# A fused attention and channel-mix kernel: batch 4's denominators by turns on VectorE too, gate-mix products and late memory keys and values on ScalarE, and a new order of steps

## The chip, the core and the metric

The kernel runs on one core of a Trainium2 chip. A core has a matrix engine (TensorE; the profile shows its products as PE and its weight loads as PEld), a vector engine (VectorE, DVE), a scalar engine (ScalarE, ACT), GpSimd (POOL), which here issues the input loads, and SyncE (SP), which issues most stores. Each engine works through its own queue in order; semaphores tie the queues together. The metric is device time in microseconds, the median of repeated executions.

## What is computed

Eight batches of eight heads, 576 positions of 64 dimensions, and 32 memory slots per head:

```python
a = exp(phi - max(phi)); a = a / (sum(a, over positions) + 1e-9)    # 8 x 8 x 576 x 32
k_m = einsum('bhsm,bhsd->bhmd', a, k);  v_m = einsum('bhsm,bhsd->bhmd', a, v)
scores = q @ k_m.T / 8
attn = exp(scores - max) / (sum(exp, over memory slots) + 1e-9)
x = (attn @ v_m), heads side by side                                # 8 x 576 x 512
x_prev = x shifted by one position, zero first
xk = mu_k * x + (1 - mu_k) * x_prev;  xr = mu_r * x + (1 - mu_r) * x_prev
kk = relu(xk @ w_k) ** 2                                            # d_ff = 1024
out = sigmoid(xr @ w_r) * (kk @ w_v)                                # float32
```

The large products are `xk @ w_k`, `kk @ w_v` and `xr @ w_r`. The kernel computes in bf16 with float32 sums, and leaves out the maxima.

## The kernel before

The order of the whole kernel is written out by hand in `PLAN` (line 19), a list of words. Each word is one step, and the steps issue their instructions in this order; an engine's queue is what the words put on it, one after the other. A word is `who:what`. `p:` is a load of weights or of the first two batches, `c0:` to `c8:` key tiles, `g:` gates, `sg:` pairs of gates, `o:` outputs, and a bare number is a step of that batch's attention. The batches run in the order 0, 1, 2, 3, 4, 5, 7, 6 up to the scores, and every step of a later batch is woven into the channel mix of earlier ones.

Attention of batch b: `exp` (line 227, ScalarE) makes exp(phi) from the loaded float32. `z` (line 249) sums it over positions by nine small products, and VectorE takes the reciprocal `rz` (line 252). `kv` (line 239) is 72 small products that give both memory keys and values in PSUM; for batches 0 and 1 keys and values are summed apart (`k`, `v`), for batch 0 also by halves of the rows (`k0c`, `k1c`, `v0c`, `v1c`). `nk` and `nv` (lines 271 and 280) multiply keys and values by `rz` on VectorE: the division of memory keys and values. `tk` turns the keys on TensorE (line 300) and copies them back (line 305). `q0`, `q1` turn the queries on VectorE (line 318). `s` makes the scores (line 333) and their exponentials (line 338, ScalarE).

The denominators are made in one of two ways. In the first, `l0` to `l3` sum the exponentials with a block of ones on TensorE (line 348) and take the logarithm on ScalarE (line 353), and `r0z`, `r1z` (or `h0z` to `h3z`) take exp(-log) (line 358). In the second, "by turns", VectorE turns the exponentials in 32 by 32 blocks (`fe`, line 363), sums and inverts them (`fs`, lines 369 and 370) and turns the result back while spreading it (`fo`, line 375). Before the change batches 0 to 4 go the first way, and 5, 6, 7 the second. `w0`, `w1` weigh the exponentials (line 382).

For batches 2 to 7, `x0` and `x1` multiply with the memory values into four PSUM tiles each, which ScalarE copies to `x` (line 394). `dd` takes the differences to the position before (line 406). The mixes `k0d`, `k2d` (for keys) and `r0d`, `r2d` (for gates) multiply two 128-row blocks of the difference by mu minus one (line 416) and add `x` (line 417), all on VectorE. Batches 0 and 1 fold mu into the memory values (`nk0` to `nr1`, line 425) and make both mixes directly by products (`mk`, `mr`, lines 287 and 442). `mub` spreads mu over the partitions (line 202), and `mu` turns it (line 210).

Channel mix: a key tile (line 514) is four products of up to 512 tokens, a Relu on ScalarE (line 518) and a square on VectorE (line 522). A gate (line 537) is four products and an Exp (line 542); `sg` ends two gates with Ln and Exp (lines 548, 549). An output is eight products (line 563), one multiply on VectorE (line 565) and its store. `busy4` issues four products of zeros (line 197), which nobody reads.

All PSUM tiles come from one ring of eight, in the order of the steps: a step that takes a tile waits until the reader of the tile eight before has finished. Inputs of batch b+2 are asked for by `b:load`, in the order phi, k, v, q, on GpSimd's queue.

Of the kernel before, what the change touches and what calls it, by code (L numbers as in the profile page):

```python
# [11 lines left out]
BF16 = mybir.dt.bfloat16  # L12
# [7 lines left out]
    "p:q:0a 0:exp1 0:exp0 0:z 0:k0c 0:mub 0:qh0 p:k:0b 0:k1c p:q:0b 0:hn1 0:hn0 p:v:0b 0:ht1 0:ht0 0:s0 0:qh1 0:s1",  # L20
    "p:v:0a 0:l0 0:l1 0:l2 0:v1c 0:h1z p:wk:0-4 0:h2z 0:nr1 0:l3 0:v0c 0:y2 0:h0z 0:nk0 0:y0 0:h3z 0:y1 0:nk1",
    "p:wr:0-4 p:wk:4-8 0:busy4 0:y3 0:nr0 0:mk1 0:mk0 p:phi:1 0:mr0 c0:1b c0:2b c0:0a c0:4a 0:mr1 p:k:1 p:q:1 c0:1a",
    "1:exp c0:7b g:2 g:3 c0:4b p:v:1 p:wv:0-2 1:z 1:k sg:1 1:nk 1:q0 g:0 c0:7a c0:3a c0:6a c0:0b g:1 1:tk 1:q1 c0:2a",
    "c0:5b c0:5a 1:s 1:v 1:nr1 1:nr0 c0:3b p:wv:2-4 1:nk0 1:l1 1:nk1 0:mu c0:6b 1:l2 1:h1z 1:l0 1:h2z 1:y1 1:y2 1:l3",
    "1:h0z o:3a o:2a 1:y0 1:h3z o:2b 1:y3 sg:0 o:3b 1:mr0 1:mk0 g:5 0:load 1:mk1 g:4 2:exp c1:1 c1:6 c1:0 2:z 1:mr1",
    "o:1b 2:kv 2:nk o:0b 2:tk 2:nv 2:q0 1:load sg:2 2:q1 c1:7 c1:2 c1:4 2:s c1:3 c1:5 3:exp 2:l2 2:l0 2:l3 o:5 2:l1",
    "2:r0z 2:r1z 2:w0 3:z 2:w1 o:1a o:4 3:kv 3:nk 3:nv 2:x0 o:0a g:8 3:tk 3:q0 2:x1 3:q1 2:dd 2:k0d g:7 g:6 3:s",
    "2:load 2:k2d sg:3 o:6 2:r0d 3:l1 o:7 3:l3 3:load 2:r2d 4:exp c2:4 3:l2 c2:6 3:l0 3:r0z c2:2 3:r1z 3:w1 4:z 3:w0",
    "c2:7 c2:0 c2:3 g:9 4:kv 3:x1 4:nv 4:nk c2:1 c2:5 3:x0 5:exp 4:tk 4:q1 4:q0 g:10 3:dd sg:4 3:k0d g:11 o:9 4:s o:8",
    "3:k2d 3:r0d sg:5 o:11 5:z 5:kv 4:l3 c3:2 4:l1 5:q1 g:12 5:nk 3:r2d 4:l2 c3:5 5:q0 4:l0 4:r1z c3:3 c3:0 5:load",  # L30
    "4:r0z 4:w1 4:w0 g:13 c3:6 5:nv sg:6 5:tk 4:load c3:7 c3:4 c3:1 4:x1 o:10 7:q1 7:q0 4:x0 o:13 4:dd 7:exp o:12",
    "4:k2d g:17 g:15 7:z 4:k0d 5:s 7:kv 5:fe 7:nk 6:exp g:14 g:16 5:fs c4:0 c4:5 4:r2d 7:nv 6:z 7:tk 5:fo sg:7 o:15",
    "5:w1 sg:8 o:14 7:s 5:w0 c4:1 c4:6 c4:4 6:kv 4:r0d 5:x0 6:nk c4:2 c4:3 7:fe c4:7 6:q0 5:x1 g:19 5:dd 6:q1 o:16",
    "o:17 g:21 6:tk 6:nv 5:k2d 5:k0d 7:fs g:18 sg:9 g:20 6:s o:18 6:fe c5:0 6:fs c5:2 c5:5 c5:3 6:fo c5:6 6:w0 6:w1",
    "c5:1 c5:4 c5:7 5:r0d 5:r2d sg:10 o:19 6:x1 o:20 7:fo o:21 7:w0 g:23 6:x0 7:w1 6:load g:22 sg:11 6:dd o:22 g:24",
    "g:25 6:k0d 7:x0 6:k2d o:23 7:x1 7:dd 6:r0d g:26 7:k0d c6:2 7:k2d 7:load c6:3 6:r2d c6:1 sg:12 c6:5 c6:7 7:r2d",
    "c6:0 c6:6 c6:4 c7:1 c7:2 c7:7 c7:4 g:27 sg:13 c7:6 o:26 c7:5 7:r0d c7:0 o:25 o:24 g:29 c7:3 o:27 c8:5 c8:1 g:31",
    "c8:0 g:30 c8:2 sg:15 g:28 sg:14 c8:7 c8:6 o:31 o:30 c8:4 g:32 g:33 o:28 c8:3 o:29 sg:16 g:35 g:34 sg:17 o:33",
    "o:32 o:34 o:35",
# [11 lines left out]
def kernel(  # L51
# [13 lines left out]
    nc = tc.nc  # L65
# [147 lines left out]
    def attention(b):  # L213
# [51 lines left out]
        def norm_k(cs=(0, 1)):  # L265

            def go():
                if "kbd" not in st:
                    st["kbd"] = work.tile([128, 2, 2, 2, PB], BF16, name="kbd", tag="kbd", bufs=3)
                for c in cs:  # L270
                    nc.vector.tensor_scalar_mul(
                        st["kbd"][:, :, c],
                        st["k"][c].rearrange("m (d h) -> m h d", h=2).unsqueeze(2).to_broadcast([128, 2, 2, PB]),
                        st["rz"][:, c:c + 1])
            return go
# [344 lines left out]
```

## Time and profile before

| | |
|---|---|
| median of 3 runs | 205.29 us (205.17 to 206.56) |
| the profiled execution | 205.91 us |
| its span, first to last instruction | 204.1 us |
| TensorE busy | 187.7 us (92%) |
| VectorE busy | 147.5 us (72%), 372 instructions |
| ScalarE busy | 148.5 us (73%), 292 instructions |
| GpSimd busy | 29.4 us (14%) |
| mean granted TensorE clock | 0.997 |
| loads and stores | 31.29 MB, 153 GB/s over the span |

Busy time is the union of an engine's instructions. A product's end is modelled, so TensorE's busy time covers the flow of products through the array. In the 40 slices, a digit is the busy share of a slice in tenths. In rows of instructions in order of time, the first number is the start in us, the second the length of the stretch; a bracket tells how long the engine had been idle and what released it. In rows of groups, after the bar stand busy us, mean ns of one, and the idle time ahead with what ended it.

### The profile page before, as it was taken

To read this page: it belongs to the slowest core of one execution; us is meant where nothing else is said; L and a number is where in the kernel's file an instruction comes from. 1 tells how busy PE (TensorE), PEld (TensorE's weight loads), DVE (VectorE), ACT (ScalarE), POOL (GpSimd) and SP (SyncE) were. 2 spreads that over 40 slices of the span, in tenths; PEclk is the share of its full clock that TensorE was granted. 3 is DMA by queue.
4 is the path that set the end of the run, shared out by engine and by line. 5 is a ranking of instruction groups with operands and counts; after the bars stand their busy time and mean duration, and the time that the engine had idled before them with its cause. 6 is when DMAs were issued, how large, how long until landed. Compare 5 with 4: busy or idle time off the path is not lost.

```text
span 204.1 us, 5371 instructions
## 1 busy us (share of the span) xinstructions
PE 187.7 (92%) x2152; PEld 98.4 (48%) x2173; DVE 147.5 (72%) x372; ACT 148.5 (73%) x292; POOL 29.4 (14%) x45
## 2 busy tenths in 40 slices
PE   0469999999999999999979999999999999999992
PEld 0225666846464454454446564444434444444451
DVE  1266747848578997997499999999999948404332
ACT  2226898998869989989839982966788493696640
POOL 7652422204123010027000000000000000000000
PEclk9999999999999999999999999999999999999998
DMA  6999999999999999789999130320532002602545
GB/s 161 179 206 207 266 207 201 265 224 283 223 264 251 243 291 211 208 135 222 265 232 230 22 91 14 92 53 3 136 71 51 0 5 51 154 0 52 119 100 143
DMA packets 24537, 31.29 MB, mean 153 GB/s; under 512 B 1968, under 2 KB 19648, under 8 KB 24512
## 3 DMA queue, kind: packets, MB, share of 16 engines
q0 software_dynamic: 17392, 20.91, 54.7%
q1 hardware_dynamic: 6352, 9.19, 17.9%
q10 hardware_dynamic: 768, 0.85, 1.3%
q8 instruction: 17, 0.28, 0.6%
q14 instruction: 8, 0.07, 0.1%
HBM read 38.28 MB, written 9.44 MB: 234 GB/s over the span
## 4 chain that ended last, share of the span: by engine, by line
PE 72%; DVE 14%; DMA 7%; ACT 3%; issue 2%; DVEq 0%; POOLq 0%
PE pk L514 24%; PE pv L563 24%; PE pr L537 13%; DMA q<-in_q_dram 4%; PE kvps L239 3%; DMA kv<-in_k_dram 3%; DVE qT L318 2%; DVE sq L522 2%; PE scps L333 2%; PE mxps L287 2%; DVE se L369 1%; PE nops L287 1%; DVE mu_d L416 1%; PE zps L348 1%; DVE o L565 1%
## 5 line engine op out<-in xcount | busy, mean ns | idle before, releaser
L514 PE MATMUL pk<-xkT,wk 128*128 128x512 bf16 (+4 forms) x346 | 67.7, 341 | 0.3
L563 PE MATMUL pv<-wv,sq 128*128 128x512 bf16 (+1 forms) x320 | 66.1, 353 | 0.4
L518 ACT ACTIVATE rl<-pk 128x512 bf16<-128x512 f32 (+3 forms) x80 | 42.4, 556 | 13.1 <-PE pk L514 7.9
L522 DVE TENSOR_TENSOR sq<-rl 128x512 bf16<-128x512 bf16 (+5 forms) x104 | 31.4, 336 | 24.3 <-ACT rl L518 23.4
L514 PEld LDWEIGHTS <-wk 128*128 128x128 bf16 x352 | 33.2, 98 | 28.4 <-issue 0.9
L563 PEld LDWEIGHTS <-sq 128*128 128x128 bf16 x328 | 31.1, 98 | 29.4 <-issue 0.9
L537 PE MATMUL pr<-wr,xrT 128*128 128x512 bf16 x137 | 34.8, 380 | 0.6 <-ACT xrT L442 0.2
L542 ACT ACTIVATE sg<-pr 128x512 f32<-128x512 f32 x36 | 21.3, 603 | 17.0 <-DVE o L565 10.0
L565 DVE TENSOR_TENSOR o<-sg,pv 128x512 f32<-128x512 f32 (+1 forms) x41 | 24.6, 614 | 10.1 <-PE pv L563 9.7
L537 PEld LDWEIGHTS <-xrT 128*128 128x128 bf16 x144 | 13.3, 98 | 14.9 <-ACT xrT L442 0.6
L549 ACT ACTIVATE sg<-sg 128x1024 f32<-128x1024 f32 x18 | 19.0, 1057 | 0.6
L548 ACT ACTIVATE sg<-sg 128x1024 f32<-128x1024 f32 x18 | 19.1, 1061 | 0.2
L394 ACT CAST x<-nops 128x320 bf16<-128x320 f32 (+1 forms) x48 | 15.6, 419 | 3.0 <-PE nops L287 3.0
L338 ACT ACTIVATE e<-scps 128x288 bf16<-128x288 f32 x32 | 10.6, 417 | 7.9 <-PE scps L333 7.9
L416 DVE TENSOR_SCALAR mu_d<-diff,mu 128x576 bf16<-128x576 bf16 x48 | 15.4, 364 | 0.1
L318 DVE STREAM_TRANSPOSE qT<-q 128x576 uint32<-128x576 uint32 (+1 forms) x16 | 13.1, 837 | 2.8 <-DMA q<-in_q_dram 2.8
L382 DVE TENSOR_TENSOR atn<-e,lz 128x576 bf16<-128x576 bf16 (+2 forms) x20 | 12.3, 631 | 1.6 <-ACT lz L358 1.6
L239 PE MATMUL kvps<-kv,em 64*32 64x128 bf16 (+1 forms) x720 | 9.0, 219 | 2.7 <-DMA kv<-in_k_dram 1.8
L227 ACT ACTIVATE em<-ph 128x1152 bf16<-128x1152 f32 (+1 forms) x9 | 9.5, 1065 | 2.5 <-DMA ph<-in_phi_dram 2.5
L239 PEld LDWEIGHTS <-em 64*32 64x32 bf16 x720 | 7.6, 96 | 6.2 <-issue 6.2
L417 DVE TENSOR_TENSOR xkT<-x,mu_d 128x1152 bf16<-128x1152 bf16 x12 | 9.1, 759 | 0.4
L417 DVE TENSOR_TENSOR xrT<-x,mu_d 128x1152 bf16<-128x1152 bf16 x12 | 9.1, 759 | 0.4
(62 smaller groups left out, 136.8 us busy)
## 6 DMA issues: line engine op xcount, KB each, us to landing
out_dram<-o SPq DMA_DIRECT2D x61, 128.0 KB, 2.4
ph<-in_phi_dram POOLq DMA_DIRECT2D x7, 576.0 KB, 17.2
kv<-in_k_dram POOLq DMA_DIRECT2D x7, 576.0 KB, 18.2
q<-in_q_dram POOLq DMA_DIRECT2D x7, 576.0 KB, 20.3
kv<-in_v_dram POOLq DMA_DIRECT2D x7, 576.0 KB, 20.5
out_dram<-o SPq DMA_DIRECT2D x18, 64.0 KB, 5.7
wk<-in_moe_w_k_dram POOLq DMA_DIRECT2D x2, 512.0 KB, 13.1
wv<-in_moe_w_v_dram POOLq DMA_DIRECT2D x2, 512.0 KB, 20.6
```

The lines of the kernel that those rows point to most:

```text
L239: nc.tensor.matmul(kvps[c][g * M:(g + 1) * M], lhsT=em[ROWS[c], j, g, :], rhs=kv5[ROWS[c], parts, g, j, :], start=j == 0, stop=j == NJ - 1 ...
L416: nc.vector.tensor_scalar_mul(t[:, i], st["d"][:, pr + i, :], mu1[:, o:o + 1])
L417: nc.vector.tensor_add(dst, st["x"][:, pr:pr + n], t)
L514: nc.tensor.matmul(pk[:, p0 - lo:p1 - lo], lhsT=wk_sb[:, di, fi * 128:(fi + 1) * 128], rhs=xk_T[:, di, p0 % RING:p0 % RING + p1 - p0], sta ...
L518: nc.scalar.activation(rl, pk, AF.Relu)
L522: nc.vector.tensor_mul(sq[:, fi, p:p + p1 - p0], rl[:, p0 - lo:p1 - lo], rl[:, p0 - lo:p1 - lo])
L537: nc.tensor.matmul(pr, lhsT=xr_T[:, di, c0:c0 + 128], rhs=wr_sb[:, di, :], start=(di == 0), stop=(di == ND - 1))
L542: nc.scalar.activation(sg[:, t % 2], pr, AF.Exp, scale=-1.0)
L548: nc.scalar.activation(gated[p], gated[p], AF.Ln, bias=1.0)
L549: nc.scalar.activation(gated[p], gated[p], AF.Exp, scale=-1.0)
L563: nc.tensor.matmul(pv[:, cols], lhsT=sq[:, fi, p:p + 128], rhs=wv_sb[:, fi, cols], start=(fi == 0), stop=(fi == NF - 1))
L565: nc.vector.tensor_mul(o[:, cols], gated[t // 2][:, t % 2, cols], pv[:, cols])
```

## The change

Three parts, and a new plan around them.

1. Batch 4 has `fe`, `fs`, `fo` in place of `l0` to `l3`, `r0z`, `r1z`: its denominators are made by turns on VectorE.
2. The gate mixes of batches 4 to 7 are `r0e`, `r2e` in place of `r0d`, `r2d`: the products with mu run on ScalarE (a Copy with a scale per partition), and the add stays on VectorE.
3. Memory keys and values of batches 4 to 7 are divided by `ak`, `av` in place of `nk`, `nv`: on ScalarE as well.

The plan orders nearly all steps anew. At the start, the second half of batch 0's keys is loaded ahead of its queries; weights `wk:4-8` come ahead of `wk:0-4`, and phi of batch 1 ahead of `wr`; `mub` and `mu` are issued ahead of batch 0's sums; the head's steps `l`, `h..z`, `s0`, `s1` are woven differently; and `busy9` stands in place of `busy4`. In the middle, `7:kv` is issued ahead of `5:s`, and `7:q0`, `7:q1` behind both values steps of batch 4. Words `6:load` and `7:load` ask for nothing, since there is no batch 8 or 9. In the plan's part of the diff below, lines of "..." stand for plan lines left out.

```diff
@@ PLAN @@
-    "p:q:0a 0:exp1 0:exp0 0:z 0:k0c 0:mub 0:qh0 p:k:0b 0:k1c p:q:0b 0:hn1 0:hn0 p:v:0b 0:ht1 0:ht0 0:s0 0:qh1 0:s1",
-    "p:v:0a 0:l0 0:l1 0:l2 0:v1c 0:h1z p:wk:0-4 0:h2z 0:nr1 0:l3 0:v0c 0:y2 0:h0z 0:nk0 0:y0 0:h3z 0:y1 0:nk1",
-    "p:wr:0-4 p:wk:4-8 0:busy4 0:y3 0:nr0 0:mk1 0:mk0 p:phi:1 0:mr0 c0:1b c0:2b c0:0a c0:4a 0:mr1 p:k:1 p:q:1 c0:1a",
-    "1:exp c0:7b g:2 g:3 c0:4b p:v:1 p:wv:0-2 1:z 1:k sg:1 1:nk 1:q0 g:0 c0:7a c0:3a c0:6a c0:0b g:1 1:tk 1:q1 c0:2a",
...
-    "3:k2d 3:r0d sg:5 o:11 5:z 5:kv 4:l3 c3:2 4:l1 5:q1 g:12 5:nk 3:r2d 4:l2 c3:5 5:q0 4:l0 4:r1z c3:3 c3:0 5:load",
-    "4:r0z 4:w1 4:w0 g:13 c3:6 5:nv sg:6 5:tk 4:load c3:7 c3:4 c3:1 4:x1 o:10 7:q1 7:q0 4:x0 o:13 4:dd 7:exp o:12",
-    "4:k2d g:17 g:15 7:z 4:k0d 5:s 7:kv 5:fe 7:nk 6:exp g:14 g:16 5:fs c4:0 c4:5 4:r2d 7:nv 6:z 7:tk 5:fo sg:7 o:15",
-    "5:w1 sg:8 o:14 7:s 5:w0 c4:1 c4:6 c4:4 6:kv 4:r0d 5:x0 6:nk c4:2 c4:3 7:fe c4:7 6:q0 5:x1 g:19 5:dd 6:q1 o:16",
...
-    "c8:0 g:30 c8:2 sg:15 g:28 sg:14 c8:7 c8:6 o:31 o:30 c8:4 g:32 g:33 o:28 c8:3 o:29 sg:16 g:35 g:34 sg:17 o:33",
-    "o:32 o:34 o:35",
+    "p:k:0b 0:exp0 0:exp1 0:mub 0:mu 0:z 0:k1c 0:k0c 0:hn0 0:hn1 p:q:0a 0:qh0 0:ht0 p:q:0b p:v:0b 0:qh1 0:ht1 p:v:0a",
+    "0:s0 0:l0 0:h0z 0:s1 0:l1 0:v0c 0:y0 0:v1c 0:nr0 0:nk1 0:h1z 0:l2 0:l3 0:nr1 p:wk:4-8 0:h3z 0:y1 0:h2z 0:y3 0:y2",
+    "0:busy9 0:nk0 p:wk:0-4 0:mk1 p:phi:1 0:mk0 c0:3b p:wr:0-4 0:mr0 1:exp 0:mr1 c0:3a c0:6b c0:1b c0:4a g:3 c0:2a",
+    "c0:5b p:k:1 g:1 g:2 1:k 1:z 1:nk p:q:1 1:q0 sg:1 1:q1 c0:7b c0:6a p:v:1 c0:7a 1:tk g:0 c0:0a c0:0b c0:5a 1:s",
...
+    "3:x1 2:r2d 4:q1 4:kv 4:ak c2:4 c2:7 3:x0 4:q0 3:load g:9 sg:4 5:exp 3:dd 4:tk 4:av 3:k2d o:8 o:9 3:k0d g:12 g:10",
+    "5:z 3:r2d 3:r0d 5:q0 4:s 5:kv 5:ak 4:fe 5:av 5:q1 g:11 c3:3 c3:0 sg:5 4:fs 5:load 7:exp c3:7 4:fo c3:6 4:w0",
+    "4:load c3:4 g:13 4:w1 o:10 c3:2 sg:6 c3:5 7:z c3:1 o:11 4:x0 g:14 7:kv 4:x1 7:ak 7:q0 7:q1 g:15 5:tk 4:dd o:12",
+    "4:k2d sg:7 5:s 4:k0d 6:exp o:13 g:16 5:fe 5:fs g:17 5:fo c4:1 7:tk sg:8 o:15 7:av c4:6 c4:5 5:w0 c4:0 c4:3 5:w1",
+    "6:z 6:q0 4:r2e 7:s c4:4 7:fe 6:load c4:2 c4:7 o:14 4:r0e 5:x0 o:17 6:kv 6:ak 7:fs 5:x1 5:dd 6:q1 g:18 g:19 sg:9",
+    "o:16 5:k0d 6:av g:21 g:20 6:tk 5:k2d 5:r2e o:19 6:s o:18 6:fe 5:r0e 6:fs c5:4 6:fo c5:2 c5:1 sg:10 g:23 6:w1",
...
+    "o:24 c7:7 o:25 g:29 7:r2e sg:13 c7:5 7:r0e o:26 c8:4 c8:3 c7:4 c8:5 c8:6 c7:3 g:28 c7:2 o:27 c8:1 sg:14 g:30",
+    "g:31 sg:15 o:31 c8:0 o:30 g:32 g:33 o:28 sg:16 c8:2 o:29 c8:7 o:33 g:35 g:34 sg:17 o:32 o:34 o:35",
@@ -262,23 +261,31 @@
                     nc.vector.tensor_sub(left, left, terms[:, i])
             st["es"] = [terms[:, i] for i in range(3)]
 
-        def norm_k(cs=(0, 1)):
+        def norm_k(cs=(0, 1), by_act=False):
 
             def go():
                 if "kbd" not in st:
                     st["kbd"] = work.tile([128, 2, 2, 2, PB], BF16, name="kbd", tag="kbd", bufs=3)
                 for c in cs:
-                    nc.vector.tensor_scalar_mul(
-                        st["kbd"][:, :, c],
-                        st["k"][c].rearrange("m (d h) -> m h d", h=2).unsqueeze(2).to_broadcast([128, 2, 2, PB]),
-                        st["rz"][:, c:c + 1])
-            return go
-
-        def norm_v():
-            vb = work.tile([128, 2, D], BF16, name="vb", tag="vb", bufs=3)
-            for c in range(2):
-                nc.vector.tensor_scalar_mul(vb[:, c], st["v"][c], st["rz"][:, c:c + 1])
-            st["vb"] = vb
+                    out, kc = st["kbd"][:, :, c], st["k"][c].rearrange("m (d h) -> m h d", h=2)
+                    kc = kc.unsqueeze(2).to_broadcast([128, 2, 2, PB])
+                    if by_act:
+                        nc.scalar.activation(out, kc, AF.Copy, scale=st["rz"][:, c:c + 1])
+                    else:
+                        nc.vector.tensor_scalar_mul(out, kc, st["rz"][:, c:c + 1])
+            return go
+
+        def norm_v(by_act=False):
+
+            def go():
+                vb = work.tile([128, 2, D], BF16, name="vb", tag="vb", bufs=3)
+                for c in range(2):
+                    if by_act:
+                        nc.scalar.activation(vb[:, c], st["v"][c], AF.Copy, scale=st["rz"][:, c:c + 1])
+                    else:
+                        nc.vector.tensor_scalar_mul(vb[:, c], st["v"][c], st["rz"][:, c:c + 1])
+                st["vb"] = vb
+            return go
 
         def head_tiles(pss, src, lo, hi, cols=slice(0, None), **flags):
             for c in range(2):
@@ -407,13 +414,16 @@
                 nc.vector.tensor_copy(d[:, :, 0:1], x[:, :, 0:1])
             return go
 
-        def mix(which, pr, n=1):
+        def mix(which, pr, n=1, by_act=False):
             def go():
                 dst = (xk_T, xr_T)[which][:, pr:pr + n, x0:x0 + S]
                 t = work.tile([128, 2, S], BF16, name="mu_d", tag="mu_d")[:, :n]
                 for i in range(n):
                     o = which * ND + pr + i
-                    nc.vector.tensor_scalar_mul(t[:, i], st["d"][:, pr + i, :], mu1[:, o:o + 1])
+                    if by_act:
+                        nc.scalar.activation(t[:, i], st["d"][:, pr + i, :], AF.Copy, scale=mu1[:, o:o + 1])
+                    else:
+                        nc.vector.tensor_scalar_mul(t[:, i], st["d"][:, pr + i, :], mu1[:, o:o + 1])
                 nc.vector.tensor_add(dst, st["x"][:, pr:pr + n], t)
             return go
 
@@ -444,7 +454,7 @@
 
         two = [(0, 0), (0, 1), (1, 0), (1, 1)]
         steps = {"exp": exp_phi, "kv": ekv(slice(0, 2)), "k": ekv(slice(0, 1)), "v": ekv(slice(1, 2)),
-                 "z": esum, "nk": norm_k(), "nv": norm_v, "tk": tr_k(), "s": scores((0, 1)), "load": reload, "mu": load_mu, "mub": load_mu_b,
+                 "z": esum, "nk": norm_k(), "nv": norm_v(), "ak": norm_k(by_act=True), "av": norm_v(True), "tk": tr_k(), "s": scores((0, 1)), "load": reload, "mu": load_mu, "mub": load_mu_b,
                  "zr": sum_rows}
         steps.update(fe=fold_e, fs=fold_sum, fo=fold_out)
         for i in range(2):
@@ -473,6 +483,7 @@
             steps[f"d{2 * i}d"] = diff(2 * i, 2)
             for w in range(2):
                 steps[f"{'kr'[w]}{2 * i}d"] = mix(w, 2 * i, 2)
+                steps[f"{'kr'[w]}{2 * i}e"] = mix(w, 2 * i, 2, by_act=True)
         steps["dd"] = diff(0, 4)
         for hf in range(2):
             steps[f"x{hf}"] = values(hf)
```

## The prediction

> **What bounds the kernel now.** I read the page first, for the engine that sets the end; then the work by stages, for where that engine is not fed; then what was waited for in the two weak places; and last the groups by shape, for prices. From the page, busy time and its 40 slices:
>
> ```profile
> PE 187.7 (92%) x2152; PEld 98.4 (48%) x2173; DVE 147.5 (72%) x372; ACT 148.5 (73%) x292; POOL 29.4 (14%) x45
> ...
> PE   0469999999999999999979999999999999999992
> ...
> DVE  1266747848578997997499999999999948404332
> ACT  2226898998869989989839982966788493696640
> ```
>
> TensorE is busy 187.7 of 204.1 us; its zeros and low digits stand only at the two ends, with a 9 nearly throughout the rest. VectorE and ScalarE have 9s in other places, so each has stages of its own in which it is full. The work by stages (columns: stretch, length, then busy us and count for PE, weight loads, DVE, ACT, POOL):
>
> ```profile
> 0.00:20.00 20.00, 9.95 (x228) 5.20 (x236) 8.36 (x28) 6.54 (x16) 11.48 (x21) 1.00 1.06 188
> ...
> 60.00:99.00 39.00, 38.63 (x490) 18.91 (x481) 35.09 (x92) 36.14 (x75) 8.22 (x11) 1.00 1.08 224
> 99.00:156.00 57.00, 55.55 (x569) 28.02 (x573) 54.05 (x122) 42.95 (x86) 0.00 (x0) 1.00 0.47 105
> ```
>
> Of TensorE's 16.4 us idle, 10.05 lie in the first 20 us and 3.9 in the last 48, most of that after its last matmul. From 60 to 99 us it loses 0.37, although ScalarE is at 36.14/39 = 93% and VectorE at 90%. From 99 to 156 it loses 1.45, with VectorE at 95% and ScalarE at 75%. So what can be won behind the start is under 3 us, whatever VectorE is spared. The wait behind most of the 1.45, from the instructions in order of time:
>
> ```profile
> 101.61 1.44 DVE L318 STREAM_TRANSPOSE qT<-q 128x576 uint32<-128x576 uint32 x2 [2.31 <-DMA q<-in_q_dram]
> ...
> 105.75 0.80 PE L239 MATMUL kvps<-kv,em 64*32 64x128 bf16 x72 [0.99 <-DVE o L565]
> ```
>
> VectorE had finished an output product at 99.3 (98.62+0.69) and stood 2.31 us until batch 7's queries landed. Behind those transposes in its queue was the product that frees the PSUM tile for batch 7's memory matmuls; TensorE stood 0.99 us for that. From 100 to 115 us TensorE is busy 13.76 of 15: 1.24 lost. The start, in order of time:
>
> ```profile
> 9.04 0.76 POOL L105 DMA_DIRECT2D ph<-in_phi_dram  x1 [0.68 <-DMA q<-in_q_dram]
> ...
> 10.24 0.67 PE L239 MATMUL kvps<-kv,em 64*32 64x64 bf16 x36 [1.06 <-DMA kv<-in_k_dram]
> ...
> 17.45 1.89 PE L197 MATMUL idle<-zeros 128*128 128x512 bf16 x4
> ...
> 19.27 2.29 PE L287 MATMUL mxps<-atn,vm 32*64 32x256 bf16 x64
> ...
> 21.50 2.46 PE L514 MATMUL pk<-xkT,wk 128*128 128x256 bf16 x16
> ```
>
> The second half of batch 0's keys comes behind the first half of its queries (GpSimd saw those landed at 9.04), so TensorE waits for it until 10.24. The four idle matmuls start 0.41 to 0.42 us apart, while 16 products of the same 512 columns at 50 to 200 us take 3.45 us, 0.216 each: TensorE is at half rate here, though the page's clock row shows 9. The 16 key products behind (eight of 256, eight of 320 columns) take 2.39 from their start to that of the next group, at 23.89; full rate would be 8x0.108+8x0.135 = 1.94. The 0.45 missing is four products of 256 columns at half rate, 0.216 for 0.108: the full clock came at about 21.5+4x0.21, near 22.3. Prices, from the groups by shape:
>
> ```profile
> L416 DVE TENSOR_SCALAR mu_d<-diff,mu 128x576 bf16<-128x576 bf16 x48 | 15.4, 364 | 0.1
> ...
> L394 ACT CAST x<-nops 128x320 bf16<-128x320 f32 x24 | 8.5, 448 | 2.4 <-PE nops L287 2.4
> ...
> L394 ACT CAST x<-nops 128x256 bf16<-128x256 f32 x24 | 7.2, 391 | 0.6 <-PE nops L287 0.6
> ...
> L271 DVE TENSOR_SCALAR kbd<-kvps,rz 128x128 bf16<-128x128 f32 x16 | 4.7, 335 | 0.3 <-PE kvps L239 0.2
> ...
> L358 ACT ACTIVATE lz<-lz 128x576 f32<-128x576 f32 x6 | 4.0, 680 | 0.1
> ...
> L280 DVE TENSOR_SCALAR vb<-kvps,rz 128x64 bf16<-128x64 f32 x12 | 2.8, 276 | 0.0
> ```
>
> **The change part by part.** *Denominators of batch 4.* Out go four column-sum matmuls (two of 320, two of 256 columns: 1152 columns at 0.216/512 = 0.49 us of TensorE), four Ln (2x0.438+2x0.384) and two Exp (2x0.680): 3.0 us of ScalarE. In comes what batches 5 to 7 already do: 0.770+1.343+0.378+1.372 = 3.86 us of VectorE. TensorE's part is on the path: **-0.49**.
>
> *Products on ScalarE.* 16 gate-mix products leave VectorE: 16x0.364 = 5.8 us. No ScalarE product with a scale per partition is in the trace. [...] I take 0.72, between 0.68 and 0.77: 11.5 us (10.9 to 12.3). [...] Keys: the casts from PSUM, 0.448 at 320 and 0.391 at 256 columns, give 0.9 ns a column, so 0.28 at 128, with the scale up to 0.37; I take 0.32 for 8, 2.6 us. Values, 64 columns: 0.27 (0.22 to 0.31) for 8, 2.2 us. VectorE is spared 8x0.335+8x0.276 = 4.9.
>
> Totals: ScalarE 148.5-3.0+11.5+2.6+2.2 = 161.8; VectorE 147.5+3.9-5.8-4.9 = 140.7. In the 57 us stage lie, by the new order, 12 products and the keys and values of two batches: ScalarE 42.95+8.6+1.3+1.1, less an Exp of memory weights that moves ahead of it (1.2), = 52.8, or 93%; VectorE 54.05-12x0.364-4x0.335-4x0.276 = 47.2, 83%. That is the load of the 60 to 99 stage, which TensorE passed with 1% idle. Each mix now has an add on VectorE behind ScalarE's products: output products and squares queue behind it, and PSUM behind those. The room is 9.8 us against six adds with at most 1.44 each; I charge **+0.3**, the loss of the 60 to 99 stage.
>
> *Middle, placed anew.* Before the transposes of batch 7's queries VectorE now has 3.86 of folds more and two key and two value steps less (2x(0.67+0.55) = 2.4): 1.4 more, so it comes at about 100.7 and stands 0.9 instead of 2.3. The loads of batch 7 wait for batch 5's memory step, which has the same TensorE work ahead (within 0.6 us), so they land as before. TensorE's 1.24 should go nearly whole: **-1.0**; bounds -1.24 and 0. What is late next: batch 4's mix for chunk 4. From its second values step to the first key tile of chunk 4 TensorE had two outputs, four gates and 1.3 us of small work, 8.2 us; now two outputs, three gates and 0.6, 6.7. The chain beneath is casts 1.5, differences 1.56, mix 1.32, an output product 0.6, mix 1.32: 6.3. It just fits.
>
> *Early part.* The transpose of mu (0.15) moves from 35.8 us to the idle start: **-0.15**. A 0.28 us stop at 41 us behind ScalarE's gate casts loses its cause, as both gates come later: **-0.2** (0 to -0.28). The other steps moved, their loads included, keep each queue's order from batch to batch; weights wk and wr change places with phi 1, and wr, landed at 19.7 before (issued 6.30, 13.4 to landing), comes about 2.6+1.6 later, 23.9. Its first gate stands behind 80 mix matmuls and five key halves, not before 25: hidden; if wr were 2 us later still, 0.9.
>
> *Start.* Second-half keys now load ahead of queries, so both key sums end at about 10.1 instead of 10.9, and the broadcast of mu is out of the way. VectorE: keys 0.56, transpose 1.36, copy 0.3, transpose 1.38, copy 0.3 from there: 14.0 for the second scores, as before (14.07). ScalarE then takes the head's Ln and Exp before the second exponentials; the last weight product ends near 18.6 and the last mu product at 19.0, 0.3 ahead of 19.27. But nine idle matmuls stand in TensorE's queue in place of four. They start at about 16.7, behind the last column sum; at 0.415 each they end at 20.4. With the full clock at 22.3 as now, TensorE has by then done 40 mix matmuls (2.23/64 = 0.035 each at half rate) and two key products; before, 64 and four. At full rate (16 took 0.35 later, 0.022; and 0.108) that is 1.1 against 1.8: +0.7. [...]
>
> **Sum.** -0.49+0.3-1.0-0.15-0.2+0.4 = -1.14. The profiled execution took 205.91, of which 204.1 are span and 1.81 around it: 204.77 by this. It stood 0.62 above the median, 205.29; from the median, **204.15**.
>
> **The rivals.** *ScalarE becomes the bound (slower).* From 99 to 156 us ScalarE also stood idle, in order, for others:
>
> ```profile
> L542 ACT ACTIVATE sg<-pr 128x512 f32<-128x512 f32 x13 | 7.7, 609 | 10.6 <-DVE o L565 5.9 <-PE pr L537 4.6
> ```
>
> With upper prices it needs 54 of the 57. If the waits for VectorE in this row (5.9) and 0.9 more of the key tiles outlive the change, it needs 60.8: TensorE loses 3.8 instead of 0.3, 207.65. It decides at 3.0 us of waits kept. For it: an engine in order can't use its holes beforehand. Against: they came from a full VectorE that is now at 83%. Chance 0.25.
>
> *The stop in the middle only moves.* If batch 7's queries land 1.5 later, or casts are late behind ScalarE's new work, chunk 4 stands for that: 204.15+1.5 = 205.65. For: the chain has 0.4 of slack. Chance 0.14.
>
> [...] Chance 0.16.
>
> **How the numbers follow.** The likeliest has 0.45: 204.15, alone 203.3 to 205.5 (its unknowns: start -0.7/+0.3, the middle up to +1.0, prices). A measurement of this kernel tells about 1%, 2.05 us, from no change: only the clock case lies below 203.24 (0.16), only the ScalarE case above 207.34 (0.25), the other two within (0.59). The range reaches to both, 202.8 to 207.9, leaving out half of each outer case.
>
> **What would show it.** Right: ScalarE near 162 and VectorE near 141 us; products at 0.68 to 0.77; TensorE's 100 to 115 us above 14.5; from 99 to 156 ScalarE about 93%, TensorE above 98%; first mix matmuls at about 20.4 behind idle matmuls 0.415 apart. Wrong: idle time of TensorE behind ScalarE's casts or Relu in that stage, VectorE's mix adds waiting above a microsecond each, a stop at chunk 4's first key tile, or a start that loses over 2 us.

## The result, and the profile after

The changed kernel takes 204.23 us (median of 9 runs, 203.78 to 204.69), against 205.29 for the kernel before, run beside it: a ratio of 0.9947 (0.9922 to 0.9973). It is faster by half a per cent, which is real by the interval and under the one per cent that the forecast called "no change". The profiled execution took 204.69, of which 202.9 are span. The forecast was 204.15 for the median and 204.77 for the profiled execution.

The page of the changed kernel, busy time and slices:

```profile
PE 188.7 (93%) x2174; PEld 97.5 (48%) x2174; DVE 143.2 (71%) x344; ACT 159.9 (79%) x318; POOL 29.5 (15%) x45
...
PE   0459999999999999999999999999999999999992
...
DVE  2275746775748999999899989898999732713422
ACT  2235989988968999999999889988999739697360
```

TensorE still sets the end. ScalarE has gained 11.4 us and VectorE has lost 4.3. Of the chain of waits that ended last, TensorE now holds 91% of the span (72% before) and VectorE 2% (14% before). The same stretches as before (length, then busy us and count for PE, weight loads, DVE, ACT, POOL):

```profile
0.00:20.00 20.00, 10.27 (x205) 5.19 (x205) 8.52 (x29) 6.92 (x15) 11.47 (x21) 1.00 1.05 198
...
60.00:99.00 39.00, 39.00 (x511) 19.32 (x510) 36.96 (x91) 35.75 (x74) 8.33 (x11) 1.00 1.11 234
99.00:156.00 57.00, 57.00 (x580) 28.36 (x579) 53.12 (x112) 53.39 (x110) 0.00 (x0) 1.00 0.45 99
```

From 60 to 156 us TensorE loses nothing. In the profile of before these two stretches show 0.37 and 1.45 us without TensorE, but its records lack 21 products of the channel mix (2152 products for 2173 weight loads; after the change 2174 for 2174). Run 2 has the order of before up to 99 us and all its products on record:

```profile
60.00:99.00 39.00, 39.00 (x455) 18.77 (x444) 35.03 (x91) 36.54 (x76) 8.22 (x11) 1.00 1.07 224
```

So the 0.37 was no loss. From 99 to 156 us the profile of before has two waits of TensorE of any size, 0.99 for the stop in the middle and 0.20 for turned memory keys, and run 2 still has the second of them.

ScalarE is at 53.39/57 = 94% in the second stretch, near the 93% forecast; VectorE is also at 93%, where 83% was forecast. From 100 to 115 us TensorE is busy 15.00 of 15 (13.76 before). The place of the old stop, VectorE in order of time:

```profile
98.86 0.68 DVE L576 TENSOR_TENSOR o<-sg,pv 128x512 f32<-128x512 f32 x1
99.83 1.44 DVE L325 STREAM_TRANSPOSE qT<-q 128x576 uint32<-128x576 uint32 x2 [0.29 <-DMA q<-in_q_dram]
```

VectorE waits 0.29 us for batch 7's queries, where it waited 2.31. It finished the output product ahead of them at 99.54, little later than before (99.31). The queries landed at 99.81, in the kernel before at 101.59: GpSimd issued their load at 90.96, for 93.18 before. This load fills the tile that held batch 5's queries (two tiles serve the batches in turn), so it can't start until VectorE has turned those. VectorE had turned them at 90.67, for 92.88 before.

Instructions by shape, for the prices:

```profile
L424 ACT ACTIVATE mu_d<-diff,mu 128x576 bf16<-128x576 bf16 x16 | 11.6, 783 | 0.0
L426 DVE TENSOR_SCALAR mu_d<-diff,mu 128x576 bf16<-128x576 bf16 x32 | 10.2, 362 | 0.0
...
L427 DVE TENSOR_TENSOR xrT<-x,mu_d 128x1152 bf16<-128x1152 bf16 x12 | 9.0, 751 | 3.7 <-ACT mu_d L424 3.4
...
L273 ACT ACTIVATE kbd<-kvps,rz 128x128 bf16<-128x128 f32 x8 | 2.6, 391 | 0.8 <-PE kvps L238 0.8
```

A gate-mix product is 0.783 us on ScalarE and 0.362 on VectorE. The 16 together take 11.6, since their records overlap a little (16 times 0.783 would be 12.5). The adds behind them waited 3.4 us in the whole kernel. The same rows for the stretch from 99 to 156 us alone:

```profile
L553 ACT ACTIVATE sg<-pr 128x512 f32<-128x512 f32 x13 | 7.6, 613 | 0.2 <-DVE o L576 0.2
...
L427 DVE TENSOR_TENSOR xrT<-x,mu_d 128x1152 bf16<-128x1152 bf16 x6 | 4.5, 742 | 0.5 <-ACT mu_d L424 0.3
```

ScalarE's gate exponentials now stand 0.2 us for VectorE's output products, where they stood 5.9. This was most of the wait that the slower rival needed; the 0.9 of key tiles behind squares is gone too. The start, TensorE in order of time:

```profile
8.96 0.99 PE L238 MATMUL kvps<-kv,em 64*32 64x64 bf16 x72 [2.19 <-DMA kv<-in_k_dram]
...
16.28 4.05 PE L196 MATMUL idle<-zeros 128*128 128x512 bf16 x9
20.26 0.70 PE L294 MATMUL mxps<-atn,vm 32*64 32x256 bf16 x40
21.17 0.69 PE L525 MATMUL pk<-xkT,wk 128*128 128x256 bf16 x4 [0.21 <-ACT xkT L452]
```

The second half of the keys landed at 8.92 and TensorE finished the sums at 9.95, about 0.95 earlier than before. The nine idle products start 0.427 us apart, at half rate as forecast (the output products of the same 512 columns start 0.216 apart), and take 4.05 us; the mix products start at 20.26 (forecast: about 20.4). In the clock records of this execution the clock is full from 20.33.

### The profile page after: what moved, and what is told of

Same layout as the page of the kernel before. It is cut to its first block, busy times and chain, and to the rows that moved or that the text cites. A ratio compares the mean times of both kernels' runs of the same rounds, so it can differ in the third digit from the quotient of the medians.

```text
span 202.9 us, 5384 instructions
## 1 busy us (share of the span) xinstructions
PE 188.7 (93%) x2174; PEld 97.5 (48%) x2174; DVE 143.2 (71%) x344; ACT 159.9 (79%) x318; POOL 29.5 (15%) x45
## 4 chain that ended last, share of the span: by engine, by line
PE 91%; DMA 3%; DVE 2%; ACT 1%; issue 1%; POOL 1%; POOLq 0%; DVEq 0%
PE pv L574 31%; PE pk L525 31%; PE pr L548 16%; PE kvps L238 4%; DMA kv<-in_k_dram 3%; PE scps L340 2%; PE idle L196 2%; PE nops L294 2%; PE mxps L294 1%; PE zps L355 1%; PE zps L248 1%; DVE qT L325 1%; DVE o L576 0%; PE ktps L307 0%; ACT e L345 0%
## 5 line engine op out<-in xcount | busy, mean ns | idle before, releaser
L525 PE MATMUL pk<-xkT,wk 128*128 128x512 bf16 (+4 forms) x352 | 68.4, 340 | 0.2 <-ACT xkT L452 0.2
L574 PE MATMUL pv<-wv,sq 128*128 128x512 bf16 (+1 forms) x328 | 67.8, 353 | 0.3 <-DVE sq L533 0.3
L529 ACT ACTIVATE rl<-pk 128x512 bf16<-128x512 f32 (+3 forms) x80 | 41.7, 559 | 10.2 <-PE pk L525 9.0
L548 PE MATMUL pr<-wr,xrT 128*128 128x512 bf16 x144 | 35.5, 379 | 0.1
L424 ACT ACTIVATE mu_d<-diff,mu 128x576 bf16<-128x576 bf16 x16 | 11.6, 783 | 0.0
L426 DVE TENSOR_SCALAR mu_d<-diff,mu 128x576 bf16<-128x576 bf16 x32 | 10.2, 362 | 0.0
```

The source lines that it names most:

```text
L525: nc.tensor.matmul(pk[:, p0 - lo:p1 - lo], lhsT=wk_sb[:, di, fi * 128:(fi + 1) * 128], rhs=xk_T[:, di, p0 % RING:p0 % RING + p1 - p0], sta ...
L529: nc.scalar.activation(rl, pk, AF.Relu)
L548: nc.tensor.matmul(pr, lhsT=xr_T[:, di, c0:c0 + 128], rhs=wr_sb[:, di, :], start=(di == 0), stop=(di == ND - 1))
L574: nc.tensor.matmul(pv[:, cols], lhsT=sq[:, fi, p:p + 128], rhs=wv_sb[:, fi, cols], start=(fi == 0), stop=(fi == NF - 1))
```

## The experiments

Every kernel below was timed in five rounds, beside the kernel before, which had medians of 205.44 (runs 1 to 4), 205.46 (5 to 8) and 205.67 us (9 to 12). Ratios are to that. "Delay" is worked out from two traces: the start of a TensorE group in one, less the start of the same group in the other. Where it grows, TensorE has stopped or does extra work. Differences between starts, which vary from execution to execution by over a microsecond (the nine idle products start at 15.60 us in run 4 and at 16.96 in run 6), stay in it as a constant.

### 1. Four idle products in the changed kernel

```diff
-    "... 0:busy9 0:nk0 p:wk:0-4 ..."
+    "... 0:busy4 0:nk0 p:wk:0-4 ..."
```

> The changed kernel with four idle products in place of nine, all else the same. Theory of the prediction: the nine products end behind the moment at which the mix products could start and cost at half rate, unless they bring the full clock earlier. In the changed kernel's profile the clock was full from 20.3 us of the span, the first mix products came at 20.26; without the five idle products they can start near 18.7. [...]

Measured: 203.86 us (203.05 to 206.36), 0.9936 (0.9899 to 0.9973). TensorE in this kernel, in order of time:

```profile
16.10 1.88 PE L197 MATMUL idle<-zeros 128*128 128x512 bf16 x4
18.49 0.70 PE L295 MATMUL mxps<-atn,vm 32*64 32x256 bf16 x40 [0.51 <-DVE vm L436]
19.84 0.61 PE L526 MATMUL pk<-xkT,wk 128*128 128x256 bf16 x4 [0.66 <-DMA wk<-in_moe_w_k_dram]
```

The mix products start 1.8 us earlier and then wait for other things: 0.51 for VectorE and 0.66 for the second half of `wk`. The 40 mix products take 0.70 us, as in the changed kernel. The intervals of this run and the changed kernel lie over each other, so the number of idle products cannot be told apart here. Run 10 tries it once more.

### 2. The order of before, with batch 7's queries turned later

```diff
-    "... 4:x1 o:10 7:q1 7:q0 4:x0 o:13", "4:dd 7:exp o:12 ..."
+    "... 4:x1 o:10 4:x0 o:13", "4:dd 7:q1 7:q0 7:exp o:12 ..."
```

> The kernel before with one move: the two transposes of batch 7's queries stand behind the differences of batch 4 in place of ahead of its values steps. Theory of the prediction: the stop of VectorE for the queries (2.31 us) and with it TensorE's 1.24 us from 100 to 115 us go; the ratio to the kernel before is 0.994 to 0.996 (1.0 us less). Rival, the stop only moves: batch 4's mixes or batch 5's scores are late, and the ratio is 1.000.

Measured: 204.77 us (204.32 to 205.2), 0.9963 (0.9939 to 0.9987), 0.7 below the kernel before. VectorE in order of time:

```profile
102.36 0.17 DVE L407 COPY diff<-x 128x4 bf16<-128x4 bf16 x1
102.42 1.43 DVE L318 STREAM_TRANSPOSE qT<-q 128x576 uint32<-128x576 uint32 x2
```

The wait for the queries is gone. The delay against the kernel before stands at -0.38 from 46 to 102 us and at -1.28 from 108 on: 0.90 won at the old stop, nothing elsewhere. So two words moved by a few places give the larger part of what the whole change gives, 0.7 of 1.1 us by the times.

### 3. The three parts in the order of before

In the plan of before, the gate mixes, keys and values of batches 4 to 7 take the words `r0e`, `r2e`, `ak`, `av`, and batch 4's denominators are placed so:

```diff
-    "... 5:kv 4:l3 c3:2 4:l1 5:q1 g:12 5:nk 3:r2d 4:l2 c3:5 5:q0 4:l0 4:r1z", "c3:3 c3:0 5:load", "4:r0z 4:w1 4:w0 ..."
+    "... 5:kv 4:fe c3:2 5:q1 g:12 5:ak 3:r2d 4:fs c3:5 5:q0 c3:3 c3:0 5:load", "4:fo 4:w1 4:w0 ..."
```

> The three parts of the change in the order of the kernel before: batch 4's denominators by turns, mix products of batches 4 to 7 and memory keys and values of batches 4 to 7 on ScalarE, no step moved. Theory of the prediction: 0.49 us less for TensorE, 0.3 more for waits behind ScalarE, the stop for batch 7's queries as before or 1 us longer for VectorE since the folds of batch 4 stand ahead: 205.0 to 205.6, ratio 0.999 to 1.002. Rival, the gain is in the parts, since VectorE is spared: ratio 0.994 to 0.996. Rival, the parts need the new order and ScalarE is the bound in the old one: ratio above 1.01.

Measured: 209.87 us (209.2 to 210.8), 1.0216 (1.0176 to 1.0256): the parts alone are slower by 4.4 us. The 205.0 to 205.6 of the prediction's sum was missed, and the ratio is that of the last rival. TensorE:

```profile
98.40 0.32 PE L295 MATMUL nops<-atn,vb 32*64 32x256 bf16 x8 [1.88 <-ACT rl L530]
```

The longest of its waits ends at batch 4's value products. The weight loads ahead of them waited 2.37 us until VectorE had weighed the exponentials, so here the denominators by turns came too late for this place. Against the kernel before the delay grows by 2.2 between 92 and 96 us (times of the kernel before), and by 2.8 between 114 and 126. It falls by 0.5 ahead of that, where the four column sums are gone, and by 1.0 behind 102, where VectorE comes later to the queries and waits 1.31 for them. So part of the gain shows in this kernel too, and more than all of it is lost.

### 4. Gate-mix products back on VectorE, in the new order

The same for batches 5, 6 and 7:

```diff
-    "... 4:r2e ... 4:r0e ..."
+    "... 4:r2d ... 4:r0d ..."
```

> The changed kernel with the gate-mix products of batches 4 to 7 back on VectorE (16 products of 0.362 us there in place of 0.783 us on ScalarE), all else the same. VectorE has 53.1 us of the 57 from 99 to 156 us and gets 12 x 0.362 = 4.3 more: 57.4. Theory of the prediction: VectorE is then full in the stage, but its mixes can be late by some microseconds, so TensorE loses 0 to 0.7: ratio to the kernel before 0.995 to 0.998. Rival, the move of the products is what the gain comes from: ratio 1.000 or above.

Measured: 204.35 us (203.39 to 205.88), 0.9949 (0.992 to 0.9978): no different from the changed kernel. VectorE is busy 147.6 us in all, as before the change, ScalarE 150.6. TensorE loses 0.21 from 99 to 156 us, where ScalarE is at 44.90 and VectorE at 55.23 of 57. The largest part of the change, by engine time, is worth nothing by itself that these times can tell.

### 5. The changed kernel once more

> The changed kernel itself, beside the others of this job: the ratio of before, 0.995 (0.992 to 0.997), so that the others can be set against it on the same chip.

Measured: 204.35 us (203.78 to 205.81), 0.9959 (0.9931 to 0.9988). The result repeats, and runs 6 to 12 are held against this one. Against the first profile of the changed kernel its delay is -0.96 at 36 us and -0.91 at 187: all of the difference is in the start.

### 6. The new order alone

In the new plan, `r0e`, `r2e`, `ak`, `av` become `r0d`, `r2d`, `nk`, `nv` for batches 4 to 7, and for batch 4's denominators:

```diff
-    "... 4:fe 5:av 5:q1 g:11 c3:3 c3:0 sg:5 4:fs 5:load 7:exp c3:7 4:fo c3:6 4:w0 ..."
+    "... 4:l0 4:l1 5:nv 5:q1 g:11 c3:3 c3:0 sg:5 4:l2 4:l3 4:r0z 5:load 7:exp c3:7 4:r1z c3:6 4:w0 ..."
```

> The new order with all three parts undone: batch 4's denominators by column sums and Ln and Exp, mix products of batches 4 to 7 and memory keys and values on VectorE, each where the new step stood. If the gain is the order's: TensorE has 0.49 us more than in the changed kernel and the ratio to the kernel before is 0.995 to 0.998. If it comes from the parts, VectorE being spared: VectorE has 53.1 us of 57 from 99 to 156 us and gets 4.3 + 2.4 more, 59.8, TensorE stands for 1 to 3 us of it, and the ratio is 1.002 to 1.012.

Measured: 207.88 us (206.82 to 208.37), 1.0128 (1.009 to 1.0167): the order alone is slower by 2.4 us. TensorE, at its longest wait:

```profile
137.28 1.04 PE L549 MATMUL pr<-wr,xrT 128*128 128x512 bf16 x4 [1.00 <-DVE xrT L428]
```

Against the changed kernel its delay grows by 1.18 between 85 and 91 us, by 0.85 between 119 and 129, and by 1.19 between 129 and 138; elsewhere behind 36 us it stays the same to 0.03. The first place holds the four column sums (0.49 by the rows of before) and a wait of 0.23 for batch 5's values, divided on VectorE. The other two are waits for VectorE: squares, batch 6's keys, a gate mix. How full VectorE was from 118 to 140 us, and what TensorE lost in that stretch:

| kernel, all in the new order | VectorE busy of 22.00 us | TensorE lost |
|---|---|---|
| changed | 20.55 (93%) | 0.00 |
| division back on VectorE (run 9) | 21.10 (96%) | 0.00 |
| gate mixes back on VectorE (run 4) | 21.37 (97%) | 0.21 |
| all three parts undone (run 6) | 21.73 (99%) | 1.69 |

Of the 1.69, 0.16 stands ahead of a product that this run's records lack. VectorE busy over the whole kernel is 147.6 us in run 4 and 147.4 here, so the total doesn't tell. In the new order the loss goes with this stretch: at 97% there is almost none, and at 99% each thing that TensorE needs from VectorE comes late. In the order of before, though, VectorE was just as full there (21.80 in run 2), and TensorE lost nothing. So fullness alone isn't the cause, and what stands next in the queue counts too. That is argued from these five traces and not shown by an edit of its own. Which two of the three parts are needed together for the loss wasn't tried either.

### 7. Every gate-mix product made twice, in the changed kernel

```diff
                         nc.scalar.activation(t[:, i], st["d"][:, pr + i, :], AF.Copy, scale=mu1[:, o:o + 1])
+                        nc.scalar.activation(t[:, i], st["d"][:, pr + i, :], AF.Copy, scale=mu1[:, o:o + 1])
```

> The changed kernel with each of the 16 mix products on ScalarE made twice into the same tile: 16 x 0.783 = 12.5 us more for ScalarE, 9.4 of them between 99 and 156 us, where it then has 62.8 us of work for 57. It measures ScalarE's room. If ScalarE is nearly the bound already (the slower rival): all 9.4 reach the end, 213 us, ratio 1.04. By the prediction's sum the room in the stage is 3.6 us, and lateness of the mixes can take up a few more: 2 to 6 us more than the changed kernel, ratio 1.005 to 1.025.

Measured: 213.46 us (212.23 to 214.39), 1.0397 (1.0349 to 1.0444): 9.1 us slower than the changed kernel, for 11.7 us more of ScalarE (171.5 for 159.8). The expected 2 to 6 us were missed, and the rival's 213 was met. TensorE at two of its waits:

```profile
137.40 1.27 PE L549 MATMUL pr<-wr,xrT 128*128 128x512 bf16 x4 [2.01 <-DVE xrT L428]
138.46 3.82 PE L526 MATMUL pk<-xkT,wk 128*128 128x512 bf16 x10
```

The first waits for a gate mix's add on VectorE, which had itself waited 1.50 us for ScalarE's products. Right behind this stop TensorE's products are slower: the second row's ten take 3.82 us, where eight take 1.89 at 184.45 and two more would add 0.43, and the first row's four take 1.27, where four take 1.03 at 181.25. The granted clock is 0.97 from 99 to 156 us, and 1.00 from 60 to 99 and from 156 on. So some 1.7 of the loss in this execution (1.5 and 0.24) is put down to the clock. Of the six executions three, at 213.84 to 214.39 us, have this one's mean granted clock of 0.992, and three, at 212.23 to 213.08, have 0.996 to 1.000, so the drop seems to have come in half of them. Without it the loss is 8.2 us (212.59, the middle of those three, against 204.35), or 8.4 by the two traces: some 70% of the added ScalarE time. The delay grows at four places (119 to 124, 129 to 138, 153 to 158, 173 to 178 us), each at or right behind a pair of doubled mixes, and not at all between 36 and 84, where this kernel differs in nothing. The changed kernel loses no TensorE time to ScalarE, but it stands close to it. From 99 us to the end of the same work, ScalarE is idle 3.7 of 57.0 us in run 5 and 4.2 of 65.5 here: the doubled products came on top of its idle time, and not into it.

### 8. Batch 4's denominators by column sums again, in the changed kernel

```diff
-    "... 4:fe 5:av ... sg:5 4:fs 5:load 7:exp c3:7 4:fo c3:6 ..."
+    "... 4:l0 4:l1 5:av ... sg:5 4:l2 4:l3 4:r0z 5:load 7:exp c3:7 4:r1z c3:6 ..."
```

> The changed kernel with batch 4's denominators back on TensorE and ScalarE (four column sums, four Ln, two Exp in the places of the three folds), all else the same. Theory of the prediction: TensorE has 0.49 us more and nothing else reaches the end: ratio to the kernel before 0.997 (0.4 to 0.6 us slower than the changed kernel). Rival: the folds, 3.86 us of VectorE ahead of batch 4's weights, cost as much as they save, and the time is the changed kernel's or less, ratio 0.994 or below.

Measured: 204.95 us (204.46 to 205.84), 0.9983 (0.9958 to 1.0008), 0.6 above run 5. Against the changed kernel the delay grows by 0.63 between 85 and 91 us, where the column sums stand, and by 0.28 between 95 and 100, where TensorE waits for a Relu. This part is worth what TensorE doesn't have to do, and a little of ScalarE.

### 9. Memory keys and values divided on VectorE again, in the changed kernel

The same for batches 5, 6 and 7:

```diff
-    "... 4:ak ... 4:av ..."
+    "... 4:nk ... 4:nv ..."
```

> The changed kernel with memory keys and values of batches 4 to 7 divided on VectorE again (8 x 0.335 + 8 x 0.276 = 4.9 us more there), all else the same. The new order with all parts undone took 207.9, with the mix products alone undone 204.35, with the denominators alone undone 204.95. If VectorE's total is what counts, this is like the mix products, 204.3 to 204.9, ratio 0.995 to 0.998. If the place counts (in the new order the division stands on VectorE's queue behind a product of TensorE that is not yet done, and ahead of transposes and output products), the loss of the order alone is here: 206 to 208, ratio 1.003 to 1.013.

Measured: 204.28 us (203.42 to 205.47), 0.9952 (0.9921 to 0.9983). VectorE is busy 146.0 us, and TensorE loses nothing from 99 to 156. By itself this part is worth nothing that the times can tell either.

### 10. Gate-mix products on VectorE and four idle products

The mixes of batches 5, 6 and 7 as that of batch 4:

```diff
-    "... 0:busy9 ... 4:r2e ... 4:r0e ..."
+    "... 0:busy4 ... 4:r2d ... 4:r0d ..."
```

> The changed kernel with mix products on VectorE and four idle products: the two edits that cost nothing or gained 0.3 us, together. If both stand as measured alone: 203.7 to 204.2, ratio 0.992 to 0.995, the best version so far; if the idle products only shift the moment of the full clock from run to run, 204.2 to 204.6.

Measured: 204.38 us (203.62 to 205.16), 0.9953 (0.9926 to 0.998). TensorE in order of time:

```profile
18.02 1.19 PE L295 MATMUL mxps<-atn,vm 32*64 32x256 bf16 x40 [0.48 <-DVE vm L436]
19.71 1.03 PE L526 MATMUL pk<-xkT,wk 128*128 128x256 bf16 x4 [0.51 <-ACT xkT L453]
20.68 1.19 PE L295 MATMUL mxps<-atn,vm 32*64 32x320 bf16 x40
```

Here the same 40 mix products took 1.19 us for the 0.70 of run 1, and the 16 key products at 21.97 took 2.55 for the 2.12 of run 1 at 21.42: TensorE reached its full rate later. With run 4 at 204.35, four and nine idle products can't be told apart by the time, and this isn't a better version.

### 11. Products and division on ScalarE in the order of before, denominators as before

In the plan of before, and the same for batches 5, 6 and 7:

```diff
-    "... 4:nv 4:nk ... 4:r2d ... 4:r0d ..."
+    "... 4:av 4:ak ... 4:r2e ... 4:r0e ..."
```

> The order of the kernel before with the two ScalarE parts (mix products, division of memory keys and values of batches 4 to 7), batch 4's denominators as before. The three parts in the old order took 209.9; TensorE stood 1.9 us for batch 4's weights behind the folds near 98 us and about 1.3 from 119 to 125 us for Relus and casts behind ScalarE's products. If the folds are the larger cause, this takes 206.5 to 207.5, ratio 1.006 to 1.011; if ScalarE's products are, 208.5 or more, ratio 1.015 or more.

Measured: 208.24 us (207.89 to 209.18), 1.0152 (1.0108 to 1.0195): 2.6 us slower than before, with VectorE spared 7.6 us in all, and just under the 208.5 expected of ScalarE's products as the larger cause. Against the kernel before, the delay grows by 2.8 between 114 and 126 us, as in run 3. ScalarE in this kernel, in order of time:

```profile
117.62 1.29 ACT L346 ACTIVATE e<-scps 128x288 bf16<-128x288 f32 x4
118.78 1.60 ACT L530 ACTIVATE rl<-pk 128x512 bf16<-128x512 f32 x3
120.21 1.49 ACT L425 ACTIVATE mu_d<-diff,mu 128x576 bf16<-128x576 bf16 x2
121.55 1.45 ACT L402 CAST x<-nops 128x320 bf16<-128x320 f32 x4
122.80 0.72 ACT L274 ACTIVATE kbd<-kvps,rz 128x128 bf16<-128x128 f32 x2
123.31 1.67 ACT L530 ACTIVATE rl<-pk 128x512 bf16<-128x512 f32 x3
```

ScalarE runs without a gap here, and from 110 to 125 us it is busy 14.94 of 15. Two mix products stand between the Relus of key tiles and in front of the casts of values. TensorE is busy 3.87 of the 5 us from 120 to 125; its waits there are 0.21 for a cast and 0.73 for a Relu. So the slower rival is a real mechanism: in this order ScalarE did become the bound for 12 us. The times of runs 3 and 11 have intervals that lie over each other, and their traces end 0.2 us apart, so what the denominators add to run 3 isn't settled.

### 12. The new order, with batch 7's queries turned earlier

```diff
-    "... c3:5 7:z c3:1 o:11 4:x0 g:14 7:kv 4:x1 7:ak 7:q0 7:q1 g:15 ..."
+    "... c3:5 7:q0 7:q1 7:z c3:1 o:11 4:x0 g:14 7:kv 4:x1 7:ak g:15 ..."
```

> The changed kernel with the transposes of batch 7's queries moved ahead of batch 7's sum, some 4 us of TensorE's work earlier, ahead of batch 4's values. If the stop for the queries is worth what the prediction says, VectorE stands some 3 us there for queries that land near 100 us, and TensorE 1.0 or more: 205.2 to 206.5, ratio 1.000 to 1.006. If VectorE's new room covers it: 204.2 to 204.5.

Measured: 205.56 us (204.86 to 206.85), 1.0023 (0.9994 to 1.0052): 1.2 above run 5, and the whole gain is gone. VectorE, in order of time:

```profile
98.38 1.44 DVE L326 STREAM_TRANSPOSE qT<-q 128x576 uint32<-128x576 uint32 x2 [1.03 <-DMA q<-in_q_dram]
99.74 0.13 DVE L252 RECIPROCAL rz<-zps 128x2 f32<-128x2 f32 x1
```

And TensorE in the same kernel:

```profile
99.93 0.32 PE L295 MATMUL nops<-atn,vb 32*64 32x256 bf16 x8 [0.54 <-DVE rz L252]
100.84 1.02 PE L549 MATMUL pr<-wr,xrT 128*128 128x512 bf16 x4 [0.60 <-DVE o L577]
```

VectorE stands for the queries, then turns them for 1.44 us, and the reciprocal and an output product behind them come late; both free PSUM tiles. Against the changed kernel the delay grows by 1.26 between 100 and 104 us, and by less than 0.02 anywhere else behind 41 us.

## Why the prediction was right, point by point

**The bound, and what could be won.** "What can be won behind the start is under 3 us, whatever VectorE is spared" held: the most that any kernel here won is 1.6 us (run 1), sparing VectorE 7.6 us (run 11) gave a slower kernel, and giving it 4.4 back (run 4) cost nothing. One reading under it was wrong: the 0.37 us from 60 to 99 us was products missing from the records, and no loss.

**Denominators of batch 4, -0.49.** Confirmed: undoing it costs 0.6 by the times (run 8), and by the trace 0.63 at the column sums' place and 0.28 behind a Relu.

**Products on ScalarE, +0.3 for new waits.** The prices for one instruction all came out just over their upper ends: 0.783 for a product (0.72 taken, at most 0.77), 0.391 for keys (0.32, at most 0.37), 0.315 for values (0.27, at most 0.31). What the upper ends add for the scale was the author's estimate, and no run shows it by itself; in its place the traces have 0.783 for the product beside 0.680 for the Exp of as many columns in the kernel before. The sums came out near, since records overlap: 11.6 for the sixteen products against 11.5, keys and values 4.7 together against 4.8. ScalarE's total is 159.9 against 161.8. VectorE's is 143.2 against 140.7: undoing the products gives it 4.4 us back and undoing the division 2.8 (runs 4 and 9), where the step had taken off 5.8 and 4.9. TensorE lost nothing in the stretch, so the charge of 0.3 was too high; it had been taken from the 0.37 us that were no loss. By the trace the multiply takes 2.2 times as long on ScalarE (0.783/0.362). The dearer engine did no harm in this order: with the products on VectorE (run 4) the kernel takes 204.35 us, as with them on ScalarE (run 5). In the order of before, products and division on ScalarE made it 2.6 us slower (run 11).

One size in this step was wrong. VectorE's load from 99 to 156 us was put at 47.2 and is 53.1: the sum took the spared work off the stretch of before, but in the new order other work moved in (30 squares instead of 24, for one). So the "room of 9.8 us" on VectorE was 3.9. The 14 us that ScalarE stood idle in this stretch before (57 less 42.95) were room: 10.4 us more of work cost TensorE nothing. The 3.6 us that were left, which run 7's expectation counted as room, were not: doubling the products put some 8 of 11.7 us on the path.

**Middle, -1.0.** Confirmed from both sides: +1.2 when the queries are turned early in the new order (run 12), -0.7 when they are turned late in the old one (run 2). The stop itself was 0.99 in the profile of before (the 1.24 has the 0.20 for turned keys in it), and nothing of it is left after. But the way there was another than forecast, so part of this hit is luck. VectorE was to come 1.4 us later to queries that "land as before", and to stand 0.9 instead of 2.3. It came 0.23 later (99.54 for 99.31), the queries landed 1.8 us earlier, and it stood 0.29. Their load didn't wait for batch 5's memory step, as the step had it, but for VectorE to turn batch 5's queries, and the new order does that 2.2 us earlier (90.67 for 92.88). What TensorE would lose in the new order if the queries landed as before wasn't tried. The chain to chunk 4 that "just fits" does fit: TensorE passes it without a stop.

**Early part, -0.15 and -0.2.** TensorE loses 0.74 from 20 to 60 us in the changed kernel and lost 0.59 in the profile of before (0.35 in run 2, which has all its products on record), so nothing was won in this stretch as a whole. Two small waits are new (0.21 for a cast at 21.17, 0.34 for a square at 38.00). These terms weren't tested by themselves.

**Start, +0.4.** Not settled. In the two profiles TensorE's idle time in the first 20 us is 9.73 after and 10.05 before, but nine idle products at half rate fill time without doing work. Four in place of nine (runs 1 and 10) gave differences within the intervals. When TensorE reaches its full rate varies from execution to execution. With nine idle products, the 40 mix products behind them took 0.70 us in seven of eight profiles and 0.83 in run 5. With four, they took 0.70 in run 1 and 1.19 in run 10, and the 64 in the order of before took 2.29 (before, runs 2 and 3) and 2.03 (run 11), where 64 at full rate would take 1.4 by the prediction's rows. So in these profiles the mix products met the full rate more often behind nine, but no time won by that is shown. The rows gave the step +0.7; going down from there to the +0.4 of the sum was the author's estimate, which no run shows. In its place the changed kernel's profile shows nine products at half rate, the full clock right behind them at 20.33, and 0.32 us less idle time in the first 20.

**The rivals.** ScalarE as the bound did not come true: it needed 3.0 us of kept waits, most of them in the gate exponentials' row, and 0.2 are left there. The stop moved nowhere. The clock case, with its chance of 0.16, was a full clock early enough for a time below 203.24; its gain was an estimate that no run shows. The clock was full earlier in this profile (20.33 for 22.21), but the kernel takes 204.23 us, and the earlier clock isn't shown as the cause of anything.

The sum came out within 0.1 us. Of its terms, -0.49 and -1.0 are confirmed; the charges of 0.3 and 0.4 and the two small gains came out near zero each or stay open, and they nearly cancel (-0.15-0.2+0.3+0.4 = +0.35). The two confirmed terms make -1.49 and the times -1.06, so some 0.4 us were lost elsewhere, in the start or the early part, and weren't located. The match to 0.1 us is in part luck.

**What the forecast did not see.** It treated the parts and the order as terms of a sum. They aren't, and the same sum missed run 3 by over 4 us. The order alone costs 2.4 us, the parts alone 4.4, and both together gain 1.1. In the new order any one part can be undone for 0 to 0.6 us, and all three together cost 3.5 (run 6 against run 5).

## What to carry to other kernels

Where a kernel's bounding engine is fed from in-order queues, ask first what one wait in the middle of a queue holds up behind it: here two words of the plan, placed behind a load's landing, were worth more than 16 products moved to another engine. Where the wait is for a load, look for the step that frees the load's tile as well: here it stood on the same queue. An engine's idle time in a stage is no room by itself: double the suspected work and see how much of it lands on the path. A new order written for a new division of labour must be judged with it, since here either alone was slower than the kernel before.

## What the runs showed of the hardware that was not expected

- After a stop of TensorE of 2.01 us (run 7, 135.39 to 137.40) its products ran at a lower rate, ten in 3.82 us, which cost some 1.7 us more in that execution. The granted clock was 0.97 from 99 to 156 us; by an estimate from that, it is short by as much as 3.4 us at half would make it (57 x 0.03 / 0.5). The 1.88 us stop in the profile of run 3 (96.52 to 98.40) lies in a stretch with a granted clock of 1.00 (95 to 100), and the next one (100 to 105) has 1.00 too. What makes the difference isn't shown.
- In the clock records of the profiles before and after, the stretch of full clock has the same length, 180.906 us: from 22.21 to 203.11 before and from 20.33 to 201.24 after. Behind it, in the last microseconds, the clock is granted at half.
- The nine idle products took from 2.89 us (run 8) to 4.05 (changed kernel, runs 5 and 6). In the changed kernel's profile all nine came before the clock was full.
